# Where the loads of w_in and of the queries stand: an early fetch, later queries, and moved masks and joins in a DeltaNet plus FFN kernel

## The chip, the cores and the metric

The kernel runs on one core of a Trainium2 chip. The metric is the device time of one execution in microseconds (us), given as the median over several runs. All inputs lie in the device's memory, and the output goes back there.

## The reference, cut to what matters

```python
# q, k, v: (4, 8, 768, 48), beta: (4, 8, 768); w_in: (384, 2048), w_out: (2048, 384)
k_n = k / (norm(k) + 1e-6)
for t in range(768):                       # a 48x48 state for each of 4 x 8 heads
    y[t]  = q[t] @ state
    v_old = state @ k_n[t]
    state = state + beta[t] * outer(k_n[t], v[t] - v_old)
x = y.transpose(0, 2, 1, 3).reshape(3072, 384)
h = x @ w_in
out = (h * sigmoid(1.702 * h)) @ w_out
```

q, k, v and beta are float32. w_in and w_out are double precision, eight bytes each: the kernel fetches the raw words and makes float32 of them itself.

## The kernel before, in words

**Units.** The recurrence is cut into chunks of 128 steps, six for each of the four batches. The 24 units of work are 24 pairs of chunk and batch. Units 0 to 3 are the first chunk of each batch (class `Step`), and here they run as two pairs, 0 and 1, then 2 and 3. Later units (class `Half`, from `slot` on, line 1333) mix two batches in one unit and run in a loop to the end, beside the FFN's matrix products. Only the front of the kernel, lines 1380 to 1617, is touched by the change.

**The front, in program order.** The first keys (`KN[0]` to `KN[3]`) are loaded by the queue of SyncE (SP, `sync`), then `beta` (`bI`) and the first queries (`QP`, which lie in the tiles `QW` and `TW`). VectorE (DVE) normalizes the first keys (`normalize_first`, with the squares on ScalarE, ACT). For each batch, `turn` transposes the keys (`psT` to `kT`), and `diagonal` makes the products of keys inside blocks of 32 (`psD`), which DVE multiplies by beta into `XBs`. I call these the blocks. When the last block is there, DVE transposes all of them into `NT` and `invert(0)` (line 643) inverts the 32x32 triangular blocks by a long chain of small operations on DVE; its result goes back into `XBs`.

While that runs, TensorE (PE) makes the Gram matrices (`gram`, `psG`), and for units 0 to 2 the scores: `psT` from the queries, an ACT copy into `QS`, the product `psQ`, ACT copies into `M`. `select` zeroes one triangle of `M` on GpSimd (POOL). The second keys (`KN[4]` to `KN[7]`) are loaded behind a one-element POOL copy into `KN[4]` that waits for the last block. `squares_second` squares them on ACT, between the scores of unit 0 and unit 1. `roots_second` sums them on DVE, takes the root on POOL (a power), and scales the second keys on DVE.

**The solve.** `gather` puts the values of a unit into `psV`. `merge` joins the inverted blocks in pairs (`psP`, then `psZ`, with ACT copies into `P` and `XBs`): these are the joins. Then eight hops (`hops`, line 1451; the loop at line 1478) alternate between the two units of the pair: `psU`, an ACT copy into `VU`, and `psV` of the next. `put_out` (line 1459) makes outputs and state, and ACT copies them into `xT` and `last`; small DMAs move rows of `last` into `xT`. With `xT` whole, the FFN's `hidden` (line 1079) computes `ph` = x @ w_in, then the gelu into `gT`. `feed()` emits one portion of it: three matrix products. The second pair has its own joins and hops (the loop at line 1537), with `feed()` in between.

**The weights.** w_in is fetched in quarters of 512 columns (`fetch_in`, line 224). Quarters 0 and 1 lie as raw words in the space of `w_out` (`raws`); of each, six DMAs go to the queue of POOL and six to that of SP, behind the second keys and the first values. The rest comes in single thirds of quarters (`thirds`), most of them held back by a small POOL copy (`paced`, line 1445). `conversion` (line 253) makes float32 of one piece in six steps: mask the exponent (DVE), clamp (ACT), add the sign (DVE), mask the fraction (DVE), join low and high words (DVE), scale (DVE). `fill(us)` emits so many microseconds, by the kernel's own table of costs, of that background work, so `fill` sets where conversions stand in DVE's and ACT's order. After w_in come w_out's pieces, and between them the inversion of the next chunk, `invert(1)`.

**Order.** Each engine runs its instructions in program order. `warm` emits matrix products without a use that keep PE busy. `send_blocks` writes the blocks of a unit of the next chunk to memory (`Nd`, four SP DMAs each), where `load_diagonals` reads them for `invert(1)`.

Of the kernel before, what the change touches and what calls it, by code (L numbers as in the profile page):

```python
# [18 lines left out]
def kernel(  # L19
# [21 lines left out]
    B, H, S, D = q.shape  # L41
# [3 lines left out]
    NBH = B * H  # L45
# [60 lines left out]
    def load(n, pairs, dma=nc.sync.dma_start):  # L106
        for dst, src in pairs:
            for rows, b, t in segments(n):
                dma(  # L109
                    out=place(dst, n)[rows, :, 0:D],  # L110
                    in_=src[b, :, t, :].rearrange("h p d -> p h d"),
                )
# [140 lines left out]
    def conversion(dst, raw, shape):  # L253

        lo, hi = raw[:, :, :, 0], raw[:, :, :, 1]
        ts, stt = vec.tensor_scalar, vec.scalar_tensor_tensor  # L260
        AND, OR = ALU.bitwise_and, ALU.bitwise_or
        E1 = 1 << 20
        p = dst.bitcast(I32)
        ts(p, hi, 0x7FF * E1, None, op0=AND)
        yield 0.75
        act.activation(p, p, ACT.Relu, scale=8.0, bias=low)
        yield 0.0
        stt(out=p, in0=hi, scalar=-(1 << 31), in1=p, op0=AND, op1=OR)
        yield 0.95
        ts(hi, hi, E1 - 1, E1, op0=AND, op1=OR)  # L270
        yield 0.7
        f = lo.bitcast(F32)
        stt(out=f, in0=lo.bitcast(U32), scalar=2.0**-32, in1=hi, op0=ALU.mult, op1=ALU.add)
        yield 0.95
        stt(out=dst, in0=f, scalar=2.0**-20, in1=dst, op0=ALU.mult, op1=ALU.mult)
        yield 0.95

    def pieces():

        for i in range(4):  # L280
            if i >= 2:
                for j in range(KC):
                    dst = w_in[:, j : j + 1, i * NQ : (i + 1) * NQ]
                    yield dst, thirds[(i - 2) * KC + j], (1, NQ), ("in", i * KC + j)
                continue
            for e in range(2):
                at = i * NQ + e * NPC
                raw = quarter(i)[:, :, e * NPC : (e + 1) * NPC, :]
                yield w_in[:, :, at : at + NPC], raw, (KC, NPC), ("in", 2 * i + e)
        i = 0  # L290
        while i < FC:
            f = order[i]
            if f in (4, 6):
                at = inside[f] * DM
                raw = as_raw(raws[:, at : at + 4 * DM], (2, DM))
                yield w_out[:, f : f + 2, :], raw, (2, DM), ("out", f)
                i += 2
            else:
                yield w_out[:, f : f + 1, :], None, (1, DM), ("out", f)
                i += 1  # L300
# [3 lines left out]
    def conversions():  # L304

        whole = list(pieces())

        def span(i, raw):
            kind, f = whole[i][3]
            if kind == "in":  # L310
                return (4 * NQ, 6 * NQ) if raw and f == 4 * KC - 1 else (0, 0)
            m = whole[i][2][0]
            if not raw:
                return f * DM, (f + m) * DM
            return (inside[f] * DM, (inside[f] + 2 * m) * DM) if f in inside else (0, 0)

        def clear(i, j):

            lo, hi = span(j, False)
            return all(hi <= a or b <= lo for a, b in (span(k, True) for k in range(i, j)))  # L320

        begun, clamped = {}, set()

        def begin(i):
            dst, raw, shape, name = whole[i]
            begun[i] = conversion(dst, places[name[1]] if raw is None else raw, shape)
            return next(begun[i])

        def clamp(i):
            if i in begun and i not in clamped:  # L330
                clamped.add(i)
                next(begun[i])

        last = len(whole) - 1
        yield begin(0)
        clamp(0)
        yield begin(1)
        for i in range(last + 1):
            ops = begun[i]
            yield next(ops)  # L340
            clamp(i + 1)
            yield next(ops)
            if i < last and i + 1 not in begun:
                yield begin(i + 1)
                clamp(i + 1)
            if 0 < i < last - 2 and clear(i, i + 2):
                yield begin(i + 2)
            yield next(ops)
            cost = next(ops)
            done.add(whole[i][3])  # L350
            fetches.pop(whole[i][3], lambda: None)()
            yield cost
            if i == 0:
                yield begin(2)
# [29 lines left out]
    def home(n):  # L384
        return KN[n % len(KN)]
# [166 lines left out]
    def diagonal(n):  # L552

        kT = kTs[n]
        ps = [
            pool_.tile([128, NP, BS], F32, tag=tag, name="psD")
            for pool_, tag in ((ps_seq, "seq"), (ps_acc, "acc"))
        ]
        for j in range(NP):
            for k in range(NB):  # L560
                t = slice(k * BS, (k + 1) * BS)
                for hh in range(2):
                    d = slice(hh * DP, hh * DP + D)
                    pe.matmul(
                        ps[hh][t, j, :], lhsT=kT[d, j, t], rhs=kT[d, j, t],
                        start=True, stop=True, skip_group_check=True,
                    )
        for hh in range(2):
            vec.tensor_tensor(
                XBs[:, n, hh::2], ps[hh],  # L570
                bT[:, n * H + hh : (n + 1) * H : 2].broadcast_to([128, NP, BS]), op=ALU.mult,
            )

    def by_lanes(t):

        return t.rearrange("p b h k -> p k (b h)")
# [803 lines left out]
    other_queue = pinned(nc.gpsimd.dma_start)  # L1380
    betas = beta.rearrange("b h (c k j) -> (b h) c k j", k=NB, j=BS)
    for blk in range(NB):
        sync(out=bI[blk * NBH : (blk + 1) * NBH], in_=betas[:, 0, blk, :])
    pool.memset(YB, 0.0)
    pool.affine_select(
        out=YB, in_=YB, compare_op=ALU.not_equal, fill=1.0, base=0,
        pattern=[[1, BS], [-1, BS]], channel_multiplier=0,
    )
    for i in range(B):
        pool.memset(QP[i][:, :, D:DP], 0.0)  # L1390
    half = cpool.tile([128, H], F32, name="half")
# [5 lines left out]
        pool.memset(KN[i][:, :, D:DP], 0.0)  # L1397


    for b in range(B):  # L1400
        load(b, ((QP, q),), sync)
    warm(NW)
    normalize_first()
    vec.transpose(bT, bI)
# [5 lines left out]
    for b in range(B):  # L1410
        if b + 1 < B:
            turn(b + 1)
        diagonal(b)
    vec.transpose(NT.rearrange("p i k -> p k i"), by_lanes(XBs))
    pool.tensor_copy(home(B)[0:1, 0, 0:1], XBs[0:1, B - 1, H - 1, 0:1])
    for n in range(B, 2 * B):
        load(n, ((KN, k),), sync)
    for b in range(HB):
        load_values(b, sync)
    fetch_in(0, other_queue)  # L1420
    fetch_in(1, other_queue)
    for b in range(B):
        gram(b)
    place_thirds()
# [3 lines left out]
        load_values(b, sync)  # L1428
    pair = [new_step(n) for n in range(B)]
    for s in pair[:3]:  # L1430
        if s.n == 1:
            areas = squares_second()
        next(s.scored)
        warm(NA)
        run(s.scored)
        warm(NA)
    for s in pair[:2]:
        s.select()
    for X in pair[:2]:
# [19 lines left out]
    def put_out(s):  # L1459
        s.queries()  # L1460
        s.outputs(True)
        steps.pop(s.n)
# [15 lines left out]
    for i in range(2 * NB):  # L1478
        together(*next(path))
        if i in (0, 1, 3, 5):  # L1480
            at = pair[i % 2].US[i // 2 * BS : i // 2 * BS + 1, 0:1]
            paced(at, *{0: (2, 2), 1: (3, 0), 3: (3, 1), 5: (3, 2)}[i])
        if i == 0:
            warm(NM // 2)
            run(products)
            run(scored)
            run(scaling)
        if i in (1, 2, 4, 5):
            turn(B + {1: 0, 2: 1, 4: 2, 5: 3}[i])
        if i in (3, 5, 6):  # L1490
            gram(B + {3: 0, 5: 1, 6: 2}[i])
        if i < 2 * NB - 1:
            warm(NU if i == 1 else NU // 2)
        if i in (5, 6):
            Nds.append(send_blocks(B + i - 5))
        if i > 5:
            fetch_out(i - 6, other_queue)
        fill(2.1 if i else 1.0)
    put_out(pair[0])
    merging = merge(pair[2:], area, ((ps_big, "big"), (ps_big, "big")))  # L1500
    fill(2.0)
    put_out(pair[1])
    fetch_out(2, other_queue)
    for X in pair[2:]:
        next(merging)
        X.gather()
        warm(NM // 2)
    fill(4.0)
    for at in range(B):
        for u in range(2):  # L1510
# [14 lines left out]
    def feed(n=1):  # L1525
        for _ in range(n):
            while ffn and next(ffn[0], None) is None:
                ffn.pop(0)
# [3 lines left out]
    for i in range(2 * NB):  # L1532
        if i == 0:
            for _ in range(HB):
                feed()
                next(merging)
                fill(1.5)
        together(*next(later))
        if i == 0:
            Nds.append(send_blocks(B + HB))  # L1540
        if i == 1:
            gram(B + HB + 1)
        if i == 2:
            load_diagonals(Nds + [send_blocks(B + HB + 1)])
        feed()
        fill(2.3)
# [102 lines left out]
```

## Time and profile before

| | |
|---|---|
| median of 3 runs | 699.12 us (696.87 to 701.27) |
| the profiled execution | 696.9 us, of which span 695.2 us |
| mean granted TensorE clock | 0.983 |
| PE busy | 662.7 us, 95% of the span |
| PE weight load (PEld) busy | 564.7 us, 81% |
| DVE busy | 477.9 us, 69% |
| ACT busy | 233.6 us, 34% |
| POOL busy | 272.5 us, 39% |
| PE busy in 20 to 40 us | 7.60 of 20 us |
| PE busy in 180 to 695 us | 510.75 of 515 us |

Times on the lines below are us from the start of the span. A line of the timeline gives the start, the length, the engine (SPq is SyncE as an issuer of DMAs), the line of the source (139 is a helper that emits most instructions, so the tile's name tells them apart), the operation, output <- inputs, the shape, and how many were merged. In square brackets stands how long the engine sat idle just before, and what ended it. Matrix products in float32 take two passes, so three products of `ph` show as six records.

### The profile page before, as it was taken

To read this page: it belongs to the slowest core of one execution; us is meant where nothing else is said; L and a number is where in the kernel's file an instruction comes from. 1 tells how busy PE (TensorE), PEld (TensorE's weight loads), DVE (VectorE), ACT (ScalarE), POOL (GpSimd) and SP (SyncE) were. 2 spreads that over 40 slices of the span, in tenths; PEclk is the share of its full clock that TensorE was granted. 3 is DMA by queue.
4 is the path that set the end of the run, shared out by engine and by line. 5 is a ranking of instruction groups with operands and counts; after the bars stand their busy time and mean duration, and the time that the engine had idled before them with its cause. 6 is when DMAs were issued, how large, how long until landed. Compare 5 with 4: busy or idle time off the path is not lost.

```text
span 695.2 us, 21740 instructions
## 1 busy us (share of the span) xinstructions
PE 662.7 (95%) x9292; PEld 564.7 (81%) x9292; DVE 477.9 (69%) x890; ACT 233.6 (34%) x571; POOL 272.5 (39%) x288
## 2 busy tenths in 40 slices
PE   9569899987999999999999999999999999999997
PEld 4446688854568898898998998998988988989997
DVE  5838746999688999796897996997995980200000
ACT  3437455542323323323333333233233133232111
POOL 2431553511148651752642734634414405205041
PEclk9979989998999999999999999999999999999999
DMA  6895646535234434336226335325231120000100
GB/s 92 130 176 124 145 100 185 110 61 139 77 92 94 82 73 104 65 71 132 55 53 130 74 70 103 80 59 101 58 73 35 37 62 13 19 13 4 27 0 24
DMA packets 149632, 54.61 MB, mean 79 GB/s; under 512 B 137824, under 2 KB 142656, under 8 KB 149536
## 3 DMA queue, kind: packets, MB, share of 16 engines
q1 hardware_dynamic: 146080, 45.83, 32.5%
q0 software_dynamic: 3456, 7.40, 4.7%
q8 instruction: 73, 1.20, 0.7%
q14 instruction: 23, 0.19, 0.1%
HBM read 38.37 MB, written 13.63 MB: 75 GB/s over the span
## 4 chain that ended last, share of the span: by engine, by line
PE 81%; DVE 7%; DMA 5%; issue 4%; POOL 2%; SPq 1%; ACT 0%; DVEq 0%; POOLq 0%; ACTq 0%
PE ph L139 33%; PE po L139 30%; PE four L139 7%; PE psU L139 3%; PE psR L139 2%; DMA w_out<-in_moe_w_in_dram 2%; DVE P L139 2%; PE ps_warm L139 2%; DVE w_out L139 1%; DVE YB L139 1%; PE psG L139 1%; SPq L139 1%; POOL TW L139 1%; DVE NT L139 1%; DVE w_in L139 1%
## 5 line engine op out<-in xcount | busy, mean ns | idle before, releaser
L139 PE MATMUL ph<-xT,w_in 128*128 128x256 f32 x1152 | 262.5, 385 | 3.7 <-DMA xT<-last 2.0
L139 PEld LDWEIGHTS ph<-xT,w_in 128*128 128x128 f32 x1152 | 216.6, 191 | 35.5 <-issue 3.0
L1114 POOL TENSOR_TENSOR gT<-gT 128x512 f32<-128x512 f32 x80 | 103.0, 1297 | 98.2 <-ACT gT L139 66.0
L139 PE MATMUL po<-w_out,gT 128*128 128x192 f32 (+1 forms) x720 | 140.1, 351 | 0.0
L139 DVE TENSOR_TENSOR P<-NT,YB 64x8 f32<-64x8 f32 (+13 forms) x195 | 125.9, 645 | 5.7
L139 PEld LDWEIGHTS po<-w_out,gT 128*128 128x128 f32 x720 | 119.4, 192 | 11.9 <-issue 1.5
L139 ACT ACTIVATE gT<-ph 128x512 f32<-128x512 f32 x90 | 53.7, 596 | 151.6 <-PE ph L139 150.6
L139 DVE TENSOR_REDUCE YB<-P 64x4 f32<-64x8 f32 (+13 forms) x195 | 78.4, 402 | 6.7
L139 PE MATMUL po<-TW,gT 128*128 128x192 f32 x480 | 81.8, 328 | 0.0
L139 PEld LDWEIGHTS po<-TW,gT 128*128 128x128 f32 x480 | 78.1, 190 | 0.7
L980 POOL TENSOR_SCALAR_AFFINE_SELECT M<-M 64x512 f32<-64x512 f32 x40 | 29.6, 740 | 86.4 <-ACT M L139 85.2
L139 DVE TENSOR_TENSOR o<-o,late 128x192 f32<-128x192 f32 x20 | 6.5, 355 | 68.1 <-ACT late L139 67.9
L139 ACT COPY VU<-psU 32x384 f32<-32x384 f32 x96 | 45.0, 469 | 18.1 <-PE psU L139 11.1
L139 DVE TENSOR_TENSOR VU<-VU,psR 32x384 f32<-32x384 f32 x40 | 22.1, 554 | 32.6 <-PE psR L139 31.9
L396 POOL TENSOR_TENSOR rn<-ssq,half 128x8 f32<-128x8 f32 x12 | 22.3, 1856 | 52.4 <-DVE ssq L139 52.4
L139 PEld LDWEIGHTS psU<-VU,XBs 32*32 32x32 f32 x1536 | 28.0, 106 | 18.1 <-issue 7.9
L109 POOL DMA_DIRECT2D KN<-in_k_dram x24 | 17.2, 716 | 58.4 <-PE four L139 47.1
L139 ACT COPY o<-po 128x192 f32<-128x192 f32 (+1 forms) x44 | 14.7, 333 | 74.7 <-PE po L139 72.6
L139 DVE TENSOR_TENSOR VU<-VU,four 128x384 f32<-128x384 f32 x19 | 10.4, 549 | 41.6 <-ACT M L139 41.4
L139 PE MATMUL psU<-VU,XBs 32*32 32x48 f32 x1536 | 33.0, 204 | 5.4 <-DVE w_out L139 5.0
L139 DVE TENSOR_TENSOR P<-NT 64x512 f32<-64x512 f32 (+7 forms) x45 | 30.6, 680 | 1.3
L139 DVE TENSOR_REDUCE NT<-P 64x32 f32<-64x512 f32 (+9 forms) x45 | 30.0, 668 | 1.5
(167 smaller groups left out, 749.4 us busy)
## 6 DMA issues: line engine op xcount, KB each, us to landing
VU<-in_v_dram SPq DMA_DIRECT2D x40, 96.0 KB, 3.0
out_dram<-o SPq DMA_DIRECT2D x40, 96.0 KB, 2.2
QW<-in_q_dram SPq DMA_DIRECT2D x76, 48.0 KB, 2.3
Kd<-KN SPq DMA_DIRECT2D x56, 64.0 KB, 2.2
late<-Kd SPq DMA_DIRECT2D x14, 256.0 KB, 2.8
KN<-in_k_dram POOLq DMA_DIRECT2D x30, 96.0 KB, 3.2
w_out<-in_moe_w_out_dram SPq DMA_DIRECT2D x7, 384.0 KB, 3.7
NT<-Nd SPq DMA_DIRECT2D x20, 128.0 KB, 2.7
```

The lines of the kernel that those rows point to most:

```text
L109: dma(out=place(dst, n)[rows, :, 0:D], in_=src[b, :, t, :].rearrange("h p d -> p h d"),)
L139: return lambda *a, **kw: tc.keep_in_program_order(op(*a, **kw))
L396: nc.gpsimd.tensor_tensor(rn, ssq, half, op=ALU.pow)
L980: nc.gpsimd.affine_select(out=M, in_=M, compare_op=ALU.is_gt, fill=0.0, base=0, pattern=[[0, H], [1, CH]], channel_multiplier=-1,)
L1114: (engine or nc.gpsimd).tensor_tensor(o, a, b, op=op)
```

## The change

It moves work in the front of the kernel.

- Quarter 0 of w_in is fetched at the very start: six DMAs on POOL's queue behind the two operations on `YB`, six on SP's queue behind the first keys. The DMAs of `beta` go from SP's to ACT's queue.
- The first queries are loaded behind the blocks: the one-element POOL copy now goes into `QP[0]`. SP's order behind it is queries 0 to 2, second keys, query 3, values, quarter 1 of w_in (all twelve DMAs on SP).
- The first exponent masks of the conversion (two on DVE, and one clamp on ACT) stand between the blocks of batch 2 and batch 3.
- `squares_second` stands behind the scores of units 0 to 2, and no longer between those of 0 and 1.
- The second `send_blocks` stands behind `put_out` of unit 1, and no longer in hop 6.
- In the second pair, both parts of the joins (`psP` and `psZ`) stand in front of the first product of x @ w_in, and one `feed()` before the hops is left of two. Two pairs of `warm` products get shorter, and two `fill(1.5)` become `fill(1.0)`.
- Pieces of w_in in thirds look up their raw words when they begin, since the list is not filled yet at the early start.

```diff
@@ pieces @@
-                    yield dst, thirds[(i - 2) * KC + j], (1, NQ), ("in", i * KC + j)
+                    yield dst, None, (1, NQ), ("in", i * KC + j)
@@ begin @@
-            begun[i] = conversion(dst, places[name[1]] if raw is None else raw, shape)
+            if raw is None:
+                raw = thirds[name[1] - 2 * KC] if name[0] == "in" else places[name[1]]
+            begun[i] = conversion(dst, raw, shape)
@@ the front @@
     for blk in range(NB):
-        sync(out=bI[blk * NBH : (blk + 1) * NBH], in_=betas[:, 0, blk, :])
+        beside(out=bI[blk * NBH : (blk + 1) * NBH], in_=betas[:, 0, blk, :])
...
+    fetch_in(0, other_queue)
     for i in range(B):
         pool.memset(QP[i][:, :, D:DP], 0.0)
...
-    for b in range(B):
-        load(b, ((QP, q),), sync)
     warm(NW)
     normalize_first()
...
         diagonal(b)
+        if b == HB:
+            fill(1.5)
     vec.transpose(NT.rearrange("p i k -> p k i"), by_lanes(XBs))
-    pool.tensor_copy(home(B)[0:1, 0, 0:1], XBs[0:1, B - 1, H - 1, 0:1])
+    pool.tensor_copy(QP[0][0:1, 0, 0:1], XBs[0:1, B - 1, H - 1, 0:1])
+    for b in range(B - 1):
+        load(b, ((QP, q),), sync)
     for n in range(B, 2 * B):
         load(n, ((KN, k),), sync)
+    load(B - 1, ((QP, q),), sync)
     for b in range(HB):
         load_values(b, sync)
-    fetch_in(0, other_queue)
-    fetch_in(1, other_queue)
+    fetch_in(1)
...
     for s in pair[:3]:
-        if s.n == 1:
-            areas = squares_second()
         next(s.scored)
         warm(NA)
         run(s.scored)
         warm(NA)
+    areas = squares_second()
@@ the first pair's hops @@
-        if i in (5, 6):
-            Nds.append(send_blocks(B + i - 5))
+        if i == 5:
+            Nds.append(send_blocks(B))
...
     put_out(pair[1])
+    Nds.append(send_blocks(B + 1))
     fetch_out(2, other_queue)
     for X in pair[2:]:
         next(merging)
         X.gather()
-        warm(NM // 2)
+        warm(NM // 4)
@@ the second pair's hops @@
         if i == 0:
             for _ in range(HB):
-                feed()
                 next(merging)
-                fill(1.5)
+                fill(1.0)
+            feed()
```

## The prediction

> **What bounds the kernel now.** The busy table by stretches of 20 us comes first. From 180 us to the end PE is busy 510.75 of 515 us; none of its work changes there, so any gain must arise earlier and arrive at 180 us. PE has three holes before that: 20 to 40 us (7.60 busy of 20), 80 to 100 (17.99), 140 to 180 (31.58 of 40). PE's timeline shows what ended the first two:
>
> ```profile
> 27.39 0.49 PE L139 MATMUL ps_warm<-ident 128*128 128x512 bf16 x2
> 39.38 2.08 PE L139 MATMUL psQ<-QS,kT 48*128 48x128 f32 x16 [11.50 <-ACT QS L139]
> ...
> 82.88 0.67 PE L139 MATMUL ph<-xT,w_in 128*128 128x256 f32 x2 [1.54 <-DMA xT<-last]
> 84.02 1.19 PE L139 MATMUL ph<-xT,w_in 128*128 128x256 f32 x2 [0.47 <-DMA xT<-last]
> 85.00 0.64 PE L139 MATMUL psZ<-XBs,ident 128*128 128x128 f32 x2
> 85.57 1.05 PE L139 MATMUL psZ<-P 32*32 32x16 f32 x64
> 86.55 2.93 PE L139 MATMUL ph<-xT,w_in 128*128 128x256 f32 x6
> ```
>
> 11.50 us go in one wait for ACT's copy of unit 1's queries. At the second place the waits are short, but six records of ph then take 2.93 us, against 1.56 at 91.53 us; the granted clock, us by us, is 0.50 from 84 to 90. The joins (psZ) stand behind ph, so they wait for xT too. ACT's timeline tells why its copy was late:
>
> ```profile
> 27.33 0.56 ACT L139 ACTIVATE squares<-KN 128x384 f32<-128x384 f32 x1
> 30.75 0.52 ACT L139 ACTIVATE squares<-KN 128x384 f32<-128x384 f32 x1 [2.86 <-DMA KN<-in_k_dram]
> 36.75 0.52 ACT L139 ACTIVATE TW<-KN 128x384 f32<-128x384 f32 x1 [5.48 <-DMA KN<-in_k_dram]
> 38.33 0.52 ACT L139 ACTIVATE TW<-KN 128x384 f32<-128x384 f32 x1 [1.05 <-DMA KN<-in_k_dram]
> 38.75 0.58 ACT L139 ACTIVATE QS<-psT 128x512 f32<-128x512 f32 x1
> ```
>
> The squares of the second keys stand ahead of it, and those keys land late. The reader sees the cause in the DMA view of 21 to 31 us: the keys on SP's queue (q1) share the engines with w_in on POOL's (q0).
>
> ```profile
> q0 software_dynamic: 415, 1.18, 65.2%
> q1 hardware_dynamic: 2626, 0.49, 44.1%
> ```
>
> What would be next without these squares is on DVE's timeline:
>
> ```profile
> 29.30 1.26 DVE L139 TENSOR_TENSOR P<-NT,YB 128x338 f32<-128x338 f32 x1
> ...
> 34.99 1.97 DVE L139 STREAM_TRANSPOSE XBs<-NT 128x1024 f32<-128x1024 f32 x1
> ```
>
> The inverse is whole at 36.96, while psP, its first reader, starts at 47.33: 10.37 us that PE's order costs.
>
> **Part by part.** Times are those of before, with the shift said.
>
> *Early fetch of quarter 0 (1.57 MB).* First keys: data flows on SP's queue from 2.0 us, and the last square starts at 7.35. POOL's first w_in DMA can issue at 3.65, behind YB's operations (2.39 + 1.26), and data follows about 1.5 us later, as after its issue at 19.96. By 5.2 us the 0.5 us slices add up to some 0.62 MB of the keys' 0.79. The remaining 0.17 MB now shares the engines. Bounds: +0.9 us if queues share equally (0.17 MB at 165 GB/s), +4.8 if POOL's whole half (0.79 MB) goes first. At 21 to 31 us the SP queue got 0.49 MB in 10 us, so 0.17 MB takes 3.5 instead of 1.0: **+2.5 us** on all that follows the first keys. The queries that leave the early queue stood behind the keys and give nothing back.
>
> [...]
>
> *beta on ACT's queue.* Four issues took 2.49 us on SP; on ACT they cost between nothing and that, behind the table load's end at 2.30. The first square slips from 3.95 to 4.8 at most, and the last one waits for the keys anyhow: **0**; without that cover, +0.85.
>
> *Masks between the blocks.* Two of 0.68 and 0.69 us (1.29 together at 44.93). DVE idles 1.61 us ahead of the last blocks (18.69), so they fit: **0**, up to +1.29 if that idle goes. The clamp (0.94) has ACT's idle 2.82 us before 20.61. They need quarter 0: 2.36 MB with the keys, at the 165 to 200 GB/s of the slices, lands by 14 to 17.5 us; masks start at 17.1 + 2.5 = 19.6.
>
> *Queries behind the blocks.* First issue 20.04 + 2.5 = 22.5; QW landed 3.0 to 3.8 us after issue, so 25.5 to 26.3, when psT is due (23.82 + 2.5). Cost 0 to 1. A score step then takes 2.8 us (42.01 to 44.85): M of unit 2 is done near 33.1 + 2.5, the squares (4 x 0.55) near 37.8. The second keys follow 0.59 MB of queries: 1.38 MB at 170 GB/s plus latency ends near 33, in time; values near 37, quarter 1 near 45, before DVE wants it (about 51).
>
> *Squares behind the scores.* The 11.50 us wait goes; next late is the inverse, 36.96 + 2.5, plus 0.75 for a second select that meets the DVE chain. The first one did: 1.26 us for an operation between neighbours of 0.45 and 0.57. psP thus starts near 40.2 instead of 47.33: **-7.1**. DVE's reduces (2 x 0.96) no longer wait. POOL's power (5.46) then ends near 47.6 and the second keys are scaled from 48.7 on; their transpose is due 4.4 us after psU, at 51: covered.
>
> PE idles about 3 us ahead of psP. If the clock falls, four groups of 64 small products cost 0.35 us more each (psZ 1.05 against 0.72): +1.4 at most, **+0.7** taken. [...] The trace has it at 0.50 after only 2.0 us of named waits at 82 to 84, so I keep the middle.
>
> *First hops.* DVE starts converting near 43 instead of 53.65, so ACT's clamps wait less for it (0.85 at 60.31), and one clamp leaves ACT's way at 52.69 (0.9): **-0.5** (0 to -1.5).
>
> *Joins in front of x @ w_in, and four SP writes behind.* SP's xT issues began at 78.44, behind eight writes of Nd; now at about 77.7, landing near 82.5 instead of 83.95 (81.7 to 83.2, by POOL's 2.2 and SP's 3.6 us). Before it PE now has psP, psV and both psZ up to 82.2. Then three products of ph (1.49) and psU (0.71) end at 84.7. Before, the next ph after psU started at 91.53, three products further: 91.53 - 84.7 - 1.49 = 5.3. It includes some 3.3 us of the half-speed clock (6.6 us at 0.5), which might return; bounds -2 to -5.5, **-5** taken. The fourth write moves behind put_out, and NT's reader, at 128.38, has 26 us of cover.
>
> *To 180 us.* PE is full from 84 to 128, so the shift arrives there. The DVE stretch of 116 to 179 is over 90% busy; its start (ACT's clamp at 116.26) stands behind a gelu that waits for ph, so it moves along. PE's 4.98 us wait for w_out at 164.38 stays. Emission of conversions is 1.5 - 1.0 us ahead: **0** (to -3, as w_out's fetch, whose 3.93 us wait ends at 108.87, is issued ahead of other writes).
>
> Sum: -7.1 + 0.7 - 0.5 - 5 = **-11.9**. On the profiled execution, 696.9, that is 685.0; its median stands 2.2 above (699.12), so I forecast **687.0**.
>
> **The rivals.** (a) *The gain stops at DVE*: a w_out fetch or invert(1) holds the 116 to 179 stretch, and half is lost: 693. For it: DVE's 93% and PE's 4.98; against: DVE's own chain starts 10 us earlier too. (b) *More*: that stretch gains its 3 and the keys lose only 0.9: 682. (c) *The wait is only replaced*: queries land after 10.5 us as the second keys did in 21 to 31, the scores end near 46, and 6 us go: 693. Against: POOL's queue is then empty. (d) *Slower*: the masks wait for quarter 0, and behind them on DVE stand the last blocks, NT and the whole inverse, so all engines wait. Each us past 19.6 costs one; break-even with the 11.9 is a landing at 31.5, and at 39 it gives 706. For it: w_in took up to 10.8 us from issue to landing; against: from the last issue, near 7, this is 18. (e) *Not what it says*: the new kernel's order of instructions has every move, so only idle DMA engines at the start could fail it, and that is (d).
>
> **How the numbers follow.** Forecast (683 to 691): 0.62; (a) 0.14, (b) 0.10, (c) 0.07, (d) 0.07. A measurement tells about 1% (7 us): 692.1 is the border. Faster: 0.62 + 0.10 and a fifth of (a) and (c), 0.76; slower 0.05 of (d); the rest, 0.19, within. The range, 680 to 694, takes in (b), and most of (a) and (c).
>
> **What would show it.** psP near 40 us and no wait of over 4 us for QS; the last square near 10; masks without a wait for w_out's DMA; both psZ before the first ph, and a clock of 1.0 at 84 to 90; the first psU of the second pair near 77, against 90.71; from 180 us on all times about 12 earlier. I am wrong if the keys land after 11 us, if psT waits for the queries, or if PE's waits at 150 to 180 grow by what the front gained.

## The result, and the profile after

| | before | after |
|---|---|---|
| median, runs side by side | 699.13 us (694.39 to 701.27) | 691.5 us (687.35 to 693.91) |
| ratio | 1 | 0.989, interval 0.985 to 0.994 |
| the profiled execution | 696.9 us | 687.35 us |
| its span, granted clock | 695.2 us, 0.983 | 685.7 us, 0.987 |
| PE busy, 180 us to the end | 510.75 of 515 us | 501.08 of 505 us |

The change gains 7.6 us at the median, a little over 1%. Ratios and their intervals, here and below, take in executions in the chip's fast state alone, so a ratio can differ by up to half a percent from the quotient of the medians in us. The profiled execution after is the fastest of its kernel's runs. Its lines show what can be gained. A second profile of the same kernel, below, shows where a usual run loses part of it.

The timeline of PE after the change, first at the joins of the first pair, then at those of the second (start, length, then the instruction; in brackets the idle time and what ended it):

```profile
40.08 0.72 PE L139 MATMUL psP<-XBs,gT 32*32 32x16 f32 x64 [1.42 <-DVE XBs L139]
...
42.40 0.71 PE L139 MATMUL psQ<-TW,kT 48*128 48x128 f32 x7
44.64 0.27 PE L139 MATMUL psQ<-TW,kT 48*128 48x128 f32 x1 [1.53 <-issue]
...
79.15 0.38 PE L139 MATMUL psZ<-XBs,ident 128*128 128x128 f32 x2
...
81.37 1.56 PE L139 MATMUL ph<-xT,w_in 128*128 128x256 f32 x6
82.87 0.86 PE L139 MATMUL psU<-VU,XBs 32*32 32x48 f32 x16
83.66 1.56 PE L139 MATMUL ph<-xT,w_in 128*128 128x256 f32 x6
```

The wait of 11.50 us for QS is gone, and psP starts at 40.08 instead of 47.33. In the second pair both psZ stand ahead of ph, which waits for no xT and takes 1.56 us a portion, at full clock. One line is new: the last of eight psQ products waits 1.53 us for "issue", for nothing that the profile shows as a releaser. Before, that wait was 0.31 us (at 50.37).

ACT's timeline after shows the second squares behind the last scores, with no wait for their DMA:

```profile
35.72 1.20 ACT L139 COPY M<-psQ 128x256 f32<-128x256 f32 x4 [0.80 <-PE psQ L139]
36.78 0.97 ACT L139 ACTIVATE squares<-KN 128x384 f32<-128x384 f32 x2
```

In the DMA view of 23 to 33 us after, SP's queue is the only one that carries data (queue, packets, MB, share of 16 engines). It moves 1.38 MB in 10 us, where it had 0.49 MB beside w_in on POOL's queue:

```profile
q1 hardware_dynamic: 7349, 1.38, 85.2%
```

DVE's timeline after, from the sums of the first keys to the blocks:

```profile
8.83 2.16 DVE L139 TENSOR_REDUCE z<-TW 128x8 f32<-128x384 f32 x4 [7.33 <-ACT TW L139]
...
20.48 0.49 DVE L139 TENSOR_TENSOR XBs<-psD,bT 128x128 f32<-128x128 f32 x2 [1.66 <-PE psD L139]
21.00 1.29 DVE L139 TENSOR_SCALAR w_in<-w_out 128x768 int32<-128x768 int32 x2
22.20 0.47 DVE L139 TENSOR_TENSOR XBs<-psD,bT 128x128 f32<-128x128 f32 x2
22.70 2.11 DVE L139 STREAM_TRANSPOSE NT<-XBs 128x1024 f32<-128x1024 f32 x1
```

The sums end at 10.99 us (before: 8.46); the run with beta back on SP, below, shows what held them. The masks stand between blocks that were ready: the idle 1.66 us lies ahead of them and not around them. NT starts at 22.70 (19.80), and the inverse is whole at 39.93 (36.96).

Then the gain melts in the hops. The first copy of psU to VU comes 6.2 us earlier than before (48.12 against 54.35), the second pair's first P only 1.1 us earlier (76.60 against 77.67). The table by stretches of after names the place (busy time of PE, PEld, DVE, ACT and POOL with counts, then the granted clock, DMA share and GB/s):

```profile
64.00:66.00 2.00, 2.00 (x33) 0.95 (x33) 1.10 (x2) 0.66 (x2) 0.14 (x1) 0.55 0.94 272
66.00:68.00 2.00, 2.00 (x49) 1.71 (x51) 0.00 (x0) 0.24 (x1) 0.00 (x0) 0.50 1.04 242
...
74.00:76.00 2.00, 2.00 (x64) 1.95 (x64) 1.93 (x5) 1.12 (x6) 0.00 (x0) 0.89 0.00 0
```

From 64 to 74 us PE runs at half clock. Before, it had 1.00 from 44 to 84 us.

Behind the hops the gain comes back. From the second pair's first P to the portion of ph behind the first psU it takes 7.06 us (76.60 to 83.66), where it took 13.86 (77.67 to 91.53). One portion (1.56 us) fewer lies in between, so 5.2 us are won in the stage of the joins. In the kernel before, half clock from 84 to 91 us lay in this stage; how much of the 5.2 us is due to it, the single parts below show. The next inversion starts 9.0 us earlier (119.37 against 128.38), as DVE's 3.93 us wait for a piece of w_out is 0.78 us now. The span ends 9.5 us earlier.

### The profile page after: what moved, and what is told of

Read it like the earlier page. It is cut to its first block, busy times and chain, and to the rows that moved or that the text cites. A ratio compares the mean times of both kernels' runs of the same rounds, so it can differ in the third digit from the quotient of the medians.

```text
span 685.7 us, 21725 instructions
## 1 busy us (share of the span) xinstructions
PE 663.2 (97%) x9290; PEld 564.2 (82%) x9290; DVE 478.5 (70%) x890; ACT 234.1 (34%) x571; POOL 268.7 (39%) x282
## 4 chain that ended last, share of the span: by engine, by line
PE 84%; DVE 10%; DMA 2%; issue 1%; ACT 1%; SPq 1%; DVEq 0%; ACTq 0%
PE ph L139 33%; PE po L139 31%; PE four L139 7%; PE psU L139 4%; DVE P L139 3%; PE psR L139 2%; DVE YB L139 2%; DVE w_out L139 2%; PE psG L139 1%; DVE NT L139 1%; PE ps_warm L139 1%; PE psY L139 1%; DMA KN<-in_k_dram 1%; DMA NT<-Nd 1%; DVE z L139 1%
## 5 line engine op out<-in xcount | busy, mean ns | idle before, releaser
L139 PE MATMUL ph<-xT,w_in 128*128 128x256 f32 x1152 | 259.8, 383 | 0.9 <-ACT gT L139 0.9
L139 PEld LDWEIGHTS po<-w_out,gT 128*128 128x128 f32 x720 | 119.2, 191 | 11.9 <-issue 1.2
L139 PEld LDWEIGHTS psU<-VU,XBs 32*32 32x32 f32 x1536 | 28.5, 106 | 17.2 <-issue 9.3
L109 POOL DMA_DIRECT2D KN<-in_k_dram x24 | 17.1, 715 | 58.0 <-PE four L139 56.8
```

The lines of the kernel that those rows point to most:

```text
L109: dma(out=place(dst, n)[rows, :, 0:D], in_=src[b, :, t, :].rearrange("h p d -> p h d"),)
L139: return lambda *a, **kw: tc.keep_in_program_order(op(*a, **kw))
```

## The experiments

The main theory says that what is missing is lost in the hops: PE's instructions come late behind the packets of w_in, and the wait halves the clock. The kernels on the hops call it **A**. Its rivals, and the theories on the single parts, are named with each kernel. All ratios are to the kernel before, run side by side, with 95% intervals; profile lines are of one execution of each kernel.

### Each part by itself

**Squares alone.** The kernel before, with the squares behind the scores and nothing else:

```diff
     for s in pair[:3]:
-        if s.n == 1:
-            areas = squares_second()
         next(s.scored)
...
+    areas = squares_second()
```

> The kernel before with one edit: the squares of the second keys stand behind the scores of units 0 to 2. Theory A, these squares alone made PE's 11.5 us wait: no wait for QS above 2 us, psP starts at 37 to 38 (47.33 before), and about 7 us of the 10 reach the end, so 692. The second keys still share the engines with w_in, so the squares end near 39.5 and the roots near 47, as in the changed kernel. Rival, the front gain is lost again in the hops (half clock there, as the changed kernel shows from 64 to 75 us): 696 to 699.

Measured: 0.9989 [0.9941, 1.0037], 696.9 us. PE's timeline has the next wait in line:

```profile
39.19 3.44 PE L139 MATMUL psV<-VU,ident 128*128 128x384 f32 x4 [6.11 <-DMA VU<-in_v_dram]
...
44.06 1.00 PE L139 MATMUL psP<-XBs,gT 32*32 32x16 f32 x64
```

The wait for QS is replaced by one of 6.11 us for the first values, which stand behind the second keys and beside w_in. psP gains 3.3 us instead of 7.25. So the early fetch and the order of the loads are what make the squares' move worth its full size at psP.

The same profile bears on the joins of the second pair. They stand behind ph here, as in the kernel before, yet the clock was 1.00 from 45 to 157 us:

```profile
80.05 0.67 PE L139 MATMUL ph<-xT,w_in 128*128 128x256 f32 x2 [0.74 <-DMA xT<-last]
...
84.55 1.56 PE L139 MATMUL ph<-xT,w_in 128*128 128x256 f32 x6
```

From the second pair's first P (74.94) to this portion of ph, behind the first psU, it takes 9.61 us, where the kernel before took 13.86 with the same order.

**Joins alone.** The kernel before, with the join edits of the diff (also the shorter `warm` and `fill`):

```diff
-        if i in (5, 6):
-            Nds.append(send_blocks(B + i - 5))
+        if i == 5:
+            Nds.append(send_blocks(B))
...
+    Nds.append(send_blocks(B + 1))
...
             for _ in range(HB):
-                feed()
                 next(merging)
-                fill(1.5)
+                fill(1.0)
+            feed()
```

> The kernel before with the second pair's part alone: both joins in front of the first product of x @ w_in, one portion of it before the hops, the second group of block writes behind put_out, shorter warm products, fill(1.0). Theory A, the joins cover the wait for xT and keep the clock up: no half clock at 84 to 90 us, 5 us less, 694, and up to 3 more in the DVE stretch, 691. Rival, the stretch from 116 to 179 us is bound by DVE and takes the gain back: 698 to 699.

Measured: 0.9962 [0.9917, 1.0007], 695.9 us. The profiled execution, a quick one of this kernel (688.8 us), shows on PE's timeline:

```profile
82.53 1.56 PE L139 MATMUL ph<-xT,w_in 128*128 128x256 f32 x6
84.02 0.86 PE L139 MATMUL psU<-VU,XBs 32*32 32x48 f32 x16
84.81 1.56 PE L139 MATMUL ph<-xT,w_in 128*128 128x256 f32 x6
```

There is no half clock at 84 to 91. From the second pair's first P (76.86) to the portion behind psU it takes 7.95 us. With one portion (1.56 us) taken off where two lie ahead, this stage takes 12.30 us in the kernel before, 8.05 with the squares alone, 7.95 here, and 7.06 in the changed kernel (7.69 in its repeat, below). So most of the 5.2 us won against the kernel before is the half clock and the longer waits for xT that its one profile has there. Where the clock is full, the order of the joins is worth 0.1 to 1.0 us. How often the kernel before has that half clock, and whether the joins in front prevent it, one profile can't tell. By the ratio the kernel gains 2.6 us, with an interval from 5.8 us gained to 0.5 lost.

**Squares and joins together, without the loads.** The kernel before with the edits of the two kernels above:

> The kernel before with two parts of the change only: the squares of the second keys behind the scores of the first three steps, and the join of the second half in front of the products of x. Loads, beta, masks and quarter 0 stay as before. If the parts add up, the ratio is 0.9989 times 0.9962, 0.995, 693.6 us, with PE's 6 us wait for the values ahead of psV (33 to 39 us) in the trace. If the early fetch and the late queries are needed for the joins' gain as well (DVE's queue of conversions being what sets the time to 180 us), 0.998 or more. If they aren't needed at all, 0.990.

Measured: 0.9933 [0.9893, 0.9973], 692.8 us, with the wait for the values again:

```profile
37.88 3.36 PE L139 MATMUL psV<-VU,ident 128*128 128x384 f32 x4 [5.28 <-DMA VU<-in_v_dram]
```

Adding up (0.995) is within the interval, and so is 0.990, which the whole change gives; 0.998 is not. So the gain of these two parts does not need the early fetch, and how much the loads add to it can't be told from this.

### What the early fetch costs

**beta back on SP's queue.**

```diff
-        beside(out=bI[blk * NBH : (blk + 1) * NBH], in_=betas[:, 0, blk, :])
+        sync(out=bI[blk * NBH : (blk + 1) * NBH], in_=betas[:, 0, blk, :])
```

> The changed kernel with the four DMAs of beta back on SyncE's queue, behind the first keys. In the changed kernel the last reduce of the first keys' squares ended at 10.99 us, against 8.46 before. Theory A, contention with w_in's early fetch delays the first keys: the reduce ends at 10.5 to 11.5 again, psP starts near 40, and the time is that of the changed kernel, 691.5, within 2 us. Theory B, beta's issues on ACT (three took 4.27 us) hold up the squares: the first square starts near 4 us, the reduce ends at 8.5 to 9.5, psP starts near 38, and the time falls by some 2 us to 689.5.

Measured: 0.9893 [0.9837, 0.9948], 690.5 us. ACT's timeline:

```profile
10.07 0.52 ACT L139 ACTIVATE TW<-KN 128x384 f32<-128x384 f32 x1 [2.92 <-DMA KN<-in_k_dram]
```

The last square waits 2.92 us for its keys, and the last sum ends at 11.17, no earlier than in the changed kernel. But in the changed kernel another wait holds the sums. ACT's timeline there (ACTq is ACT as an issuer of DMAs):

```profile
3.96 4.27 ACTq L139 DMA_DIRECT2D bI<-in_beta_dram  x3
8.28 0.94 ACT L139 ACTIVATE TW<-KN 128x384 f32<-128x384 f32 x2 [5.97 <-DMA bI<-in_beta_dram]
9.42 0.98 ACT L139 ACTIVATE TW<-KN 128x384 f32<-128x384 f32 x2 [0.21 <-DVE z L139]
```

No square waits for keys: the last of the first keys had landed at 7.89 us (7.27 in the kernel before, 9.98 with beta on SP), and the first square starts at 8.28, right behind the last issue. So two causes of about 2.5 us lie side by side here, ACT's issues of beta and, without them, the late keys. Taking one away leaves the other. Why three issues take 4.27 us, and why the keys are later with beta on SP, is not shown.

**Quarter 0 wholly on SP's queue, behind the keys** (with beta on SP too):

```diff
-    fetch_in(0, other_queue)
+    fetch_in(0)
```

> The changed kernel with all of quarter 0 on SyncE's queue behind the first keys and beta, none on POOL's. Theory A, the 2.5 us on the first keys come from POOL's half sharing the engines: the last reduce ends near 8.5 to 9 us (10.99 in the changed kernel), NT near 20.5, psP near 38, and if w_in lands by 18 the masks do not wait; 2 us less, 689. Rival, SyncE's issues take so long that the masks wait for w_in's last rows: NT at 22.7 or later, and no gain.

Measured: 0.9928 [0.9892, 0.9964], 692.3 us. DVE's timeline:

```profile
7.90 0.55 DVE L139 TENSOR_REDUCE z<-TW 128x8 f32<-128x384 f32 x1 [0.43 <-ACT TW L139]
...
22.11 2.08 DVE L139 STREAM_TRANSPOSE NT<-XBs 128x1024 f32<-128x1024 f32 x1
```

With beta on SP and POOL's half gone the sums end at 8.45, as before the change. The run above differs from this one only in POOL's half and ends them at 11.17, so there POOL's half beside the keys costs 2.7 us. In the changed kernel itself it is ACT's issues of beta that set the time. A kernel with beta on ACT and no half on POOL was not run. NT starts only 0.9 us earlier than in the changed kernel's repeat (22.11 against 22.99), and the time does not show a gain.

**Masks behind the blocks.** `fill(1.5)` goes from between the blocks to the `fill(3.0)` before the hops, which becomes 4.5:

```diff
         diagonal(b)
-        if b == HB:
-            fill(1.5)
...
-    fill(3.0)
+    fill(4.5)
```

> The changed kernel with the first masks behind the inverse instead of between the blocks (fill(1.5) there gone, fill(3.0) before the hops made fill(4.5)). In the changed kernel the two masks ran from 21.00 to 22.29 us between the last blocks, with no idle time around them. Theory A, they delay the inverse by their own length: NT at 21.4 and the inverse whole at 38.7 (22.70 and 39.93 with the masks), psP at 38.9, and the conversions of quarter 0 start 1.3 us later in exchange: time within 1.5 us of the changed kernel, either way. Rival, they only fill a wait for PE: NT stays at 22.7.

Measured: 0.989 [0.9827, 0.9953], 690.0 us. DVE's timeline:

```profile
21.88 2.09 DVE L139 STREAM_TRANSPOSE NT<-XBs 128x1024 f32<-128x1024 f32 x1
```

NT starts 1.1 us earlier than with the masks between (22.99 in the repeat), and the inverse is whole 1.3 us earlier (39.01 against 40.28). The masks were not hidden. At the end, the difference is less than can be measured.

### Where the hops lose

**The changed kernel once more**, with no edit:

> The changed kernel once more, beside the others on one chip. Both theories: 690 to 692 and about 1.1% below the kernel before. If PE waits for instructions at the eighth product of psQ, the wait marked issue near 43 us is there again (1.53 us in the first profile, 3.1 and 2.9 in two kernels that differ from it elsewhere), and a half-clock stretch follows somewhere between 46 and 75 us.

Measured: 0.9912 [0.9881, 0.9943], 691.7 us. Its profiled execution (693.1 us) is a usual one. PE's timeline:

```profile
46.55 0.37 PE L139 MATMUL psQ<-TW,kT 48*128 48x128 f32 x1 [3.10 <-issue]
```

The issue wait is 3.10 us here, half clock lasts from 46 to 63 us, and the second pair's first P comes at 81.50, which is 3.8 us later than before the change although psP was 6.9 us earlier.

**A third more warming products in the hops.**

```diff
-    NW, NR, NA, NY, NM, NU = 80, 11, 3, 14, 8, 12
+    NW, NR, NA, NY, NM, NU = 80, 11, 3, 14, 8, 16
```

> The changed kernel with NU 16 instead of 12: one 512-column warm product more in most hops of the first pair (about 0.2 us each at full clock, 1.5 us in all if none is hidden). Theory A, the half clock from 64 to 75 us comes from PE being idle too much in the hops: the clock stays at 1.0 there, and the time falls by 3 to 4 us to about 688. Rival, the hops are long for want of instructions (waits marked issue) and the clock only follows: the half clock stays, and the time is 691.5 to 693.

Measured: 0.9893 [0.9823, 0.9963], 692.3 us, so the gain that A expected did not come. The issue wait was 2.88 us. The clock was back after four microseconds (half from 46 to 50), and fell again at 67 after a wait of 0.88 us for kT.

**150 more PE instructions in the warming at the start.**

```diff
-    warm(NW)
+    warm(66)
+    ps = ps_moe.tile([128, 2, 256], F32, tag="moe", name="ps_warm")
+    for _ in range(82):
+        pe.matmul(ps[:, 0, 0:32], lhsT=ones[:, 0:128], rhs=ones[:, 0:32], start=True, stop=True)
     normalize_first()
```

> The changed kernel with 14 warm PE instructions less and 164 small ones more ahead of the first keys' transposes, where PE has nothing else to do: the same work with PE's instruction stream shifted by 150. In four profiles PE stalls, marked issue, at the same product of psQ, 1.2 us after a packet of the instruction queue starts, and until 2.75 us after it. Theory A, PE runs out of fetched instructions there, and the stall belongs to the place in the stream: the wait at psQ near 43 us is gone or below 0.5 us, psU follows 1.5 to 3 us earlier (near 46), and with no half clock after it the time falls by 3 to 4 us to 687.5. Rival, psQ waits there for something that the profile does not show: the wait stays at the same product, and so does the time, 691.

Measured: 0.9895 [0.9854, 0.9936], 690.3 us. PE's timeline:

```profile
43.53 0.59 PE L139 MATMUL psZ<-P 32*32 32x16 f32 x48
45.51 0.31 PE L139 MATMUL psZ<-P 32*32 32x16 f32 x16 [1.38 <-issue]
```

The wait has left psQ and stands inside psZ, 106 instructions further (53 products with their weight loads). So it went with the shift of PE's instructions and did not stay at psQ, and 106 + 150 = 256. The profiles of the kernel before and of the changed kernel show the same distance. Counted in PE's records from the start (weight loads, products and semaphore instructions), their waits marked issue between 15 and 92 us stand at 450, 705 and 1218 before and at 450, 1217 and 1986 after, each 193 or 194 behind a multiple of 256. The DMA view carries a queue named "instruction" with packets of 16 KB, 73 of them in each of the two profiles. In the changed kernel such a packet starts 2.4 to 2.8 us before each of the three waits ends (at 17.56, 41.94 and 55.36 us; the waits end at 19.96, 44.64 and 58.16), in the kernel before 2.3 to 2.7 us (at 15.78, 19.40 and 47.98; 18.18, 21.73 and 50.68). That PE waits for these packets is the author's reading; no record names them as a releaser. Half clock (46 to 60) came all the same.

**The DMA engines quiet at the joins.** Quarter 1 and the first thirds are held behind a new one-word copy on POOL that reads the first inverse:

```diff
-    fetch_in(1)
     for b in range(B):
         gram(b)
...
-    fetch_in(2, js=(0,))
...
+    pool.tensor_copy(raws[0:1, 3 * NQ * 2 : 3 * NQ * 2 + 1].bitcast(F32), inverse[0][0:1, 0, BS // 2 : BS // 2 + 1])
+    fetch_in(1)
+    fetch_in(2, js=(0,))
     paced(inverse[0][0:1, 0, BS // 2 : BS // 2 + 1], 2, 1)
```

> The changed kernel with its second quarter of w_in (quarter 1) and the first block of thirds held behind a copy on POOL that reads the first inverse, so that none of their packets moves between the inverse and the scores; the last two values go ahead of them. Theory A, PE's instructions come late because the packets of w_in take the DMA engines between 41 and 46 us: the issue wait ahead of psQ falls from 2.5 to 3.1 us to under 0.7, half clock between 46 and 64 us goes or is under 5 us long, the second pair's first P comes near 77, and DVE, which now waits for quarter 1, gives 1 or 2 us back: ratio near 0.985, 687 us. Rival, a block of instructions takes its 2.75 us whatever else the DMA engines carry: the wait stays over 2 us, the half clock stays, 691 to 693 us, up to 695 if quarter 1 comes so late that DVE's filling has nothing to convert before the hops.

The DMA view of 38 to 46 us has 0.01 MB of data on SP's queue, where the changed kernel has 1.84 MB:

```profile
q1 hardware_dynamic: 43, 0.01, 0.6%
```

PE's timeline:

```profile
43.62 0.27 PE L139 MATMUL psQ<-TW,kT 48*128 48x128 f32 x1 [0.50 <-issue]
...
61.65 0.28 PE L139 MATMUL psU<-VU,XBs 32*32 32x48 f32 x1 [7.03 <-ACT VU L139]
```

The issue wait is 0.50 us at the same place and clock, with psP at 40.09 as in the changed kernel. In the seven profiles with w_in's traffic there (the two of the changed kernel, and those with beta on SP, masks late, quarter 0 on SP, and both with more warming) it was 1.53 to 3.12. That looks like A's first half. But the kernel before and the one with squares and joins speak against it: they carried 1.1 MB in the 6 us around the wait (187 and 186 GB/s; the changed kernel 234, its repeat, which waited longer, 213) and waited 0.31 and 0.28 us; squares alone and joins alone carried 183 and 181 GB/s and had no wait there. From the start of the first psP to the end of the wait it is 3.3 us in these two, 3.5 in the quiet one, 4.6 and 6.1 in the two profiles of the changed kernel. The wait is longer where the packet of the "instruction" queue starts later: 0.65 us behind the first psP in the kernel before (47.98 against 47.33), 1.86 us in the changed one (41.94 against 40.08), and both waits end 2.70 us after the packet's start. So a packet that starts 1.21 us later goes with a wait that is 1.22 us longer. Without traffic the wait is short, then; but traffic alone does not make it long, and what starts a packet was not found. The clock stayed at 1.00 to 57 us. Then the price of the hold came. DVE's and ACT's timelines:

```profile
59.07 0.69 DVE L139 TENSOR_SCALAR w_in<-w_out 128x768 int32<-128x768 int32 x1 [9.24 <-DMA gT<-in_moe_w_in_dram]
```

```profile
59.80 0.94 ACT L139 ACTIVATE w_in<-w_in,low 128x768 int32<-128x768 int32 x1 [7.51 <-DVE w_in L139]
60.75 0.47 ACT L139 COPY VU<-psU 32x384 f32<-32x384 f32 x1
```

POOL's copy stood behind its power (5.46 us, to 47.23), so quarter 1 came late. DVE waited for it, ACT's clamp waited for DVE, and the copies of the hops stand behind the clamp. Half clock from 57 to 85 us followed. The time, 0.9999 [0.9971, 1.0026], 696.9 us, is the whole gain lost.

**More warming, and eight products more where PE waits for kT in hop 5** (with `NU` 16 too):

```diff
             turn(B + {1: 0, 2: 1, 4: 2, 5: 3}[i])
+        if i == 5:
+            warm(8)
```

> The changed kernel with a third more warming products in the hops (16 for 12, 8 for 6) and eight more behind the transpose of the second keys in hop 5, where PE waits 0.9 us for kT. Theory A, the half clock in the hops lasts because these waits follow one another: a denser PE has its full clock again by 50 us and keeps it to 80; the hops come 4 us sooner, second pair's first P near 77, ratio near 0.984, 688 us. Rival, the clock's fall is settled by the issue wait ahead of psQ and by other gaps that the warming products don't fill: half clock of 10 us or more between 46 and 80 as before, and the added products cost their own 0.5 to 1 us: 691 to 693 us.

Measured: 0.9926 [0.9884, 0.9968], 692.4 us. The kT wait went, the issue wait was 2.95 us, half clock lasted from 47 to 61 us: the rival's numbers.

**A short quiet.** The last third of quarter 1, the first thirds and the last two values stand behind a one-word copy on DVE instead:

```diff
-    fetch_in(1)
+    fetch_in(1, js=(0, 1))
...
-    fetch_in(2, js=(0,))
     for b in range(HB, B):
-        load_values(b, sync)
+        loaded[b] = VU[b % len(VU)]
...
+    vec.tensor_copy(quarter(1)[0:1, 2, 0:1, 0].bitcast(F32), half[0:1, 0:1])
+    fetch_in(1, js=(2,))
+    fetch_in(2, js=(0,))
+    for b in range(HB, B):
+        load_values(b, sync)
     paced(inverse[0][0:1, 0, BS // 2 : BS // 2 + 1], 2, 1)
```

> The changed kernel with the DMA engines emptied for the joins only: the last third of quarter 1, the first block of thirds and the last two values stand behind a one-word copy on DVE at 42 us (behind its transposes of P), so that they are issued at 42 to 48 us rather than 38 to 44, and POOL, whose 5.5 us operation held quarter 1 back to 47 us in the run before, has no part in it. Theory A (packets of w_in delay PE's instructions, and the wait they cause is what halves the clock in the hops): the issue wait ahead of psQ is under 1 us, no half clock between 44 and 57, quarter 1 is there when DVE asks for it at 50 us (wait under 1 us), the second pair's first P comes at 76 to 78, 4 us sooner than in the repeat of the changed kernel: ratio 0.986, 687.5 us. Rival 1, the short hold is too short and the wait stays over 2 us: 691 to 693 us. Rival 2, the wait goes but the clock falls at the next small gap (instructions at 55 to 58 us, or a wait for the transposed keys), so that the hops gain less than 1.5 us: 690 to 692 us.

Measured: 0.9894 [0.9856, 0.9931], 691.1 us (684.35 to 696.17): no better than the changed kernel. In the profiled execution no issue wait is left at the joins, but the clock had fallen already at 40 us, behind this wait on PE's timeline:

```profile
38.49 2.24 PE L139 MATMUL psV<-VU,ident 128*128 128x384 f32 x4 [1.40 <-DMA VU<-in_v_dram]
```

The table by stretches shows half clock beside a full PE, here in one of its rows:

```profile
44.00:46.00 2.00, 2.00 (x26) 1.10 (x30) 1.97 (x6) 0.93 (x2) 1.47 (x1) 0.50 0.03 8
```

PE is full by this table and yet at half clock for 24 us. As PE also came to its psQ later here (46.72 against 42.40 us), this run does not show that the short quiet removes the wait. It does show that half clock comes without the issue wait: A's second half falls as the one cause.

### The hops in one table

The hop stage is the time from the first copy of psU to the second pair's first P, of one profiled execution each.

| kernel | psP, us | issue wait, us | half clock, 44 to 85 us | hop stage, us |
|---|---|---|---|---|
| before | 47.33 | 0.31 | from 84 | 23.3 |
| joins alone | 47.01 | none | none | 23.3 |
| squares alone | 44.06 | none | to 45 | 24.1 |
| masks late | 39.16 | 2.52 | 46 to 60 | 27.5 |
| changed | 40.08 | 1.53 | 64 to 74 | 28.5 |
| changed, repeat | 40.41 | 3.10 | 46 to 63 | 28.9 |
| short quiet | 42.9 | none | to 64 | 29.0 |
| squares and joins | 42.36 | 0.28 | 62 to 80 | 31.8 |
| quiet | 40.09 | 0.50 | 57 to 85 | 39.0 |

The other five, all with half clock in the hops, lie between 27.3 and 30.2 us. Where half clock fell into the hops, they took 4 to 8.5 us longer (15.7 in the quiet one, with its wait of 7 us). Four kernels had a wait of 5.3 to 11.5 us before the joins and half clock behind it, to 42 to 45 us; three of them kept full clock in the hops (before, squares alone, joins alone), the fourth did not (squares and joins).

The traces' records of the clock add something. Half clock lasted 10.24 us in the changed kernel (64.19 to 74.43) and 17.1 in its repeat (46.3 to 63.4), three and five times 3.41 us. In the eleven profiles with a table us by us from 20 to 180 us (all but the quiet one, squares and joins, and the one with eight products more), every stretch of half clock is one, two, three, four, five or seven times 3.41 us long, within 0.04 us. Counted off in lengths of 3.41 us, the falls in the changed kernel and in its repeat lie 0.8 us off each other. So where a wait stands against these lengths, which differs between executions of one kernel, is a rival cause of the falls that none of the edits tests. PE's idle time does not settle it alone: in the changed kernel PE was busy for 2.00 of the 3.41 us from 36.87 to 40.28 and the clock stayed at 1.00, and for 2.47 of the 3.41 us from 60.78 to 64.19, and it fell.

No version here beats the changed kernel by more than can be told.

## Why the prediction was right, and where it was not

The forecast was 687.0 us with a range of 680 to 694; the median is 691.5. The side and the range hold. On the profiled executions the sum said -11.9 and the measure is -9.55.

- **Early fetch, +2.5: the number came out, the cause did not.** The first keys' sums end 2.53 us later. The term stood for keys that share the engines with w_in, but in the changed kernel the last of the keys landed only 0.62 us later (7.89 against 7.27). With beta on SP the sharing costs 2.7 us, so the size was right for that order of the issues. Of the 2.53 us 1.7 reached the first kT copy (15.62 against 13.89). The upper bound, +4.8, was not reached: the measured delays are 0.6 and 2.7.
- **beta on ACT, 0: this step failed, and was covered by luck.** The first square was to slip to 4.8 at most. It slipped to 8.28, as three issues took 4.27 us on ACT where four on SP had taken 2.49, and that is what set the 2.53 us. It cost nothing on top only because the keys would have been as late without it.
- **Masks, 0: wrong.** They cost 1.1 to 1.3 us, the upper bound. The row `XBs x4 [1.61]` was misread: one idle time ahead of the blocks of two batches merged in one row is not an idle time between them.
- **Queries, 0 to 1, and squares behind the scores, -7.1: psP came 7.25 us earlier.** This agreement is partly luck. The masks cost 1.2 more than the sum had, the second select's collision with the inverse nothing instead of 0.75 (from NT's start to the whole inverse it took 17.23 us against 17.16), and of the 2.5 us on the first keys some 0.8 were made good before NT.
- **Clock ahead of psP, +0.7: 0.** The term was the middle of an estimate of 0 to 1.4. psP and psZ ran at 0.72 us for 64 products, with the clock at 1.00 from 40 to 60 us in the profiled execution. It fell 24 us behind psP's start, at 64.19: in the 3.41 us ahead of that PE was busy for 2.47 us, and its longest pause was 0.94 us (62.98 to 63.92).
- **First hops, -0.5: this step failed.** They lost 5.2 us: the lead on the kernel before was 6.2 us at their start and 1.1 at their end. If PE set the pace throughout the 10.24 us at half clock, full clock would have saved half of them, 5.1 us (an estimate). The sum looked at DVE's and ACT's waits there, and took the clock for a matter of the one idle time ahead of psP. It had no term for the issue wait (1.53 us), and none for half clock in the middle of the hops, where PE is full.
- **Joins, -5: 5.2 us between these two profiles, but most of it is not shown to come from the order of the joins.** The term counted 3.3 us of half clock, seen in one profile of the kernel before, as part of the gain. Squares alone, with the old order and full clock, takes 8.05 us for the stage against 7.06 in the changed kernel and 7.95 with the joins alone, so the order is worth 0.1 to 1.0 us there. One marker given for it (the second pair's first psU near 77) did not agree with the sum's own 84; it came at 82.87.
- **To 180 us, 0 to -3: -3.2.** Behind the joins the lead was 6.3 us (the 5.2, and 1.1 left from the hops); it grew to 9.0 at the next inversion and 9.5 at the end, and the bound's reason holds: the wait for w_out's piece fell from 3.93 to 0.78 us. Nothing was stopped at DVE, so rival (a) gave nearly the time measured but not its cause.
- **Slower (d): not seen.** No mask waited for quarter 0; behind the keys it was there in time.

What stays open: why the issue wait is long in the changed kernels (1.5 to 3.1 us) and not in the four others under traffic (0.31 us at most), and what lets the clock fall in the hops. A wait of 0.9 to 3.1 us lies just ahead of most falls, but the first psP wait of 1.42 us in the changed kernel had none behind it. Filling waits, moving them and emptying the DMA engines for a short time changed where the clock falls and not the median; emptying them for longer cost the whole gain.

## What to carry to other kernels

A wait that is taken away pays only as far as the loads of its successor are in time: the squares alone gained 3.3 us of 7.25, since the values were next, so a move of work and a move of its loads are one change. An idle time in a row of merged instructions stands ahead of the first of them; look at the single ones before you put work into it. And a gain in one stage has to be followed stage by stage in a second execution, because 10.24 us of half clock went with some 5 us lost in one stage of one execution and need not stand there in another: it lay in the hops after the change and in the stage of the joins before it. And before a delay is put down to one cause, take it away and look at what waits then: the late keys and the issues of beta each hid the other.

## What the runs showed of the hardware that was not expected

PE's waits marked issue stood 193 or 194 records behind a multiple of 256 in the profiles before and after (three waits each), and 150 more instructions ahead of it moved the wait at psQ on by 106. There, in a stage of 64-product groups, PE stood for 0.3 to 3.1 us in eleven profiles and not at all in three. In the profiles before and after the six waits ended 2.3 to 2.8 us after a packet of 16 KB on the queue named "instruction" started, and the later packet went with the longer wait (1.86 us behind psP and 1.53 us, against 0.65 and 0.31).

Half clock lasted 3.4 to 23.9 us in the eleven profiles with a table us by us, in whole multiples of 3.41 us, and stood also beside a full PE in the stage of small products (0.50 with 2.00 of 2 us busy, 44 to 46 us of the short quiet). It fell behind waits as short as 0.9 us (0.94 us, to 63.92, in the changed kernel). In the four sets of 17 to 25 runs of the kernel before that lie beside the experiments, time and mean granted clock have correlations of -0.78 to -0.92, with 3.6 to 6.0 us for 0.01 of clock. The medians of the clock are alike before and after (0.98). So most of the spread between executions goes with the clock, while the difference of the two kernels does not.
